# A sliding-window attention block: the row maxima's two bf16 halves written by ScalarE and GpSimd instead of VectorE

## The chip, the cores and the metric

The kernel runs on one core of a Trainium2 chip. A core has five engines with a queue of instructions each, worked off in order: TensorE (PE, with its weight loads as PEld), VectorE (DVE), ScalarE (ACT), GpSimd (POOL) and SyncE (SP, which here only issues DMA transfers). They meet through semaphores. The metric is the device time of one execution in microseconds, the median of several; lower is better.

## The reference

One transformer block on x of 2048 x 640, in f32: a layer norm, then attention and a gated MLP in parallel, and the sum of both with x.

```python
def _A_ref(x, wqkv, wo):                    # H = 32 heads of Dh = 20, window W = 256
    qkv = (x @ wqkv).reshape(B, S, 3, H, Dh).transpose(2, 0, 3, 1, 4)
    q, k, v = qkv[0], qkv[1], qkv[2]
    scores = einsum("bhqd,bhkd->bhqk", q, k) * (Dh ** -0.5)
    scores = where(mask, scores, -1e9)      # 0 <= query - key < 256
    p = softmax(scores, axis=-1)
    o = einsum("bhqk,bhkd->bhqd", p, v)
    return o.transpose(0, 2, 1, 3).reshape(B, S, D) @ wo

def _B_ref(x, w_gate, w_up, w_down):
    return (gelu(x @ w_gate) * (x @ w_up)) @ w_down

xn = _layernorm(x)
return x + _A_ref(xn, wqkv, wo) + _B_ref(xn, w_gate, w_up, w_down)
```

The softmax subtracts each row's maximum before the exponential. That maximum is what the change is about.

## The kernel before, in words

The work comes in three stages. Up to about 60 us: the layer norm, its turn by TensorE and the first projections. From 60 to about 560 us: the attention, with the rest of the projections and part of the MLP as filler. After that: the rest of the MLP and the output products.

The attention goes over 32 units, eight groups of four heads times four chunks of 512 queries. `qs` and `ks` are the stacks of a unit's q and k in SBUF: bf16 parts of q and k in 60 rows each way (q and k are split into upper and lower bf16 parts so that the product is nearly exact), and four rows more (rows 60 to 63). In those four rows the q stack holds the row maximum as two bf16 numbers, an upper part and the rest (rows 60 and 61) and zeros; the k stack holds constants (`ones`, rows 60 and 61) and zeros. A product over all 124 rows then gives score minus maximum at no further cost.

The maxima are taken a unit or more ahead. `max_pair` (line 509) multiplies 32 queries at a time with their 288 keys into PSUM (`ps_m`, line 529), and VectorE adds the mask and takes the maximum of each row (line 533; two rows of the profile each, the reduction into `junk` and the reading of its accumulator into `mx`). Eight pairs make a unit's 16 columns of `mx`. Behind the eighth, the function `negate` writes the two bf16 halves with their sign into `nm` (lines 542 and 543), and line 544 turns `nm` in blocks of 32 x 32 into `mr`, so that queries lie along a row. `max_end` (line 548) copies `mr` into the q stack by four DMA transfers on SP's queue (line 552).

`exp_piece` (line 573) multiplies the stacks (`ps_e`, line 587) and ScalarE takes the exponential into `P` (line 589); `clear` masks the edges on GpSimd (lines 600 and 603); `av_unit` multiplies `P` with v (`ps_o`, line 627), ScalarE copies the two halves out (lines 631 and 632) and GpSimd adds them (line 633). Filler: `save_qk` splits a projection (`pt` and `r`: line 285 on ScalarE, 281 on VectorE, 266 on ScalarE, 267 on GpSimd), `gate_up_fill` computes the MLP's gate (674, 675, 684 on ScalarE; 680, 688, 695 on VectorE), `split_later` splits weights (656, 661), and `x_sums` forms sums on GpSimd (758).

All queues are in the order in which the code is written. `attention` (line 823) counts slots, 14 to a unit (`NS`): in slots 0, 4 and 8 it takes pairs of maxima (four pairs in slot 0, two before and two behind `av_unit`), in slots 2, 4, 6, 8 and 10 score pieces (three, two, two, two, three), loads the k stack three units ahead in slot 9 and the q stack in slot 12, and puts some 2.4 steps of filler behind each slot. `defer(n, fn)` runs fn at the start of the slot n later, `late(fn)` behind the slot's score pieces. The eighth pair of a unit falls into slot 0 of the unit before it, behind `av_unit`; `negate` runs there. `max_end` comes six slots later. PSUM for `ps_m`, `ps_e` and `ps_o` is a ring of six banks: a piece writes the bank that was used six banks before, once its reader has finished.

Of the kernel before, what the change touches and what calls it, by code (L numbers as in the profile page):

```python
# [13 lines left out]
AF = mybir.ActivationFunctionType  # L14
OP = mybir.AluOpType
# [56 lines left out]
def block_kernel(ctx, tc, x, wqk, wv, wgu, wdo, wdl, out):  # L72
    nc = tc.nc
# [64 lines left out]
    def ln_load(t, lp):  # L138
        xi = lp.tile([128, D], F32, name="xi", tag="xi", bufs=8)
        nc.sync.dma_start(xi, x[t * 128:(t + 1) * 128, :])  # L140
        return xi
# [53 lines left out]
    now = [None]  # L195

    def at(slot, fn, *a):
        acts.setdefault(slot, []).append((fn, a))
# [17 lines left out]
    def late(fn, *a):  # L216
        if now[0] is None or now[0] < NS:
            fn(*a)
        else:
            lates.append((fn, a))  # L220
# [9 lines left out]
    def defer(n, fn, *a):  # L230
        if now[0] is None:
            fn(*a)
        else:
            at(now[0] + n, fn, *a)
# [8 lines left out]
    def load_qk(t):  # L243
        raw = wrp.tile([128, KT, 128], F32, name="wr", tag="wr")
        nc.sync.dma_start(raw, wqk[t])
        return raw
# [43 lines left out]
    def load_v(h, res, rpool=None):  # L290
        wh = wvp.tile([128, KT, 320], F32R, name="wvh", tag="wvh")
        wl = wvp.tile([128, KT, 320], F32R, name="wvl", tag="wvl")

        if rpool is not None:
            rall = rpool.tile([128, KT, 320], F32, name="wvall")
            nc.sync.dma_start(rall, wv[h])

        def get(k):
            if rpool is not None:
                return rall[:, k, :]  # L300
            raw = wvp.tile([128, 320], F32, name="wvr", tag="wvr", bufs=2)
            nc.sync.dma_start(raw, wv[h, :, k, :])
            return raw
        raws = [get(0), get(1)]
        yield
        for k in range(KT):
            if rpool is None and 0 < k < KT - 1:
                raws.append(get(k + 1))
            nc.scalar.activation(wh[:, k, :], raws[k], AF.Copy)
            nc.gpsimd.tensor_tensor(out=wl[:, k, :], in0=raws[k], in1=wh[:, k, :].bitcast(F32), op=OP.subtract)  # L310
            if rpool is not None and k + 2 < KT:
                raws.append(get(k + 2))
            yield
        res.append((wh, wl, v_tiles()))
# [26 lines left out]
    def run(*gens):  # L341
        for gen in gens:
            for _ in gen:
                pass
# [84 lines left out]
    with tc.tile_pool(name="lp", bufs=1, side="right") as lp:  # L429
        xs = [ln_load(t, lp) for t in range(2)]  # L430
        wr0 = load_qk(0)
        xs += [ln_load(t, lp) for t in range(2, 4)]
        warm = lp.tile([128, 256], BF, name="warm")[:, 0:128]
        nc.vector.memset(warm, 0.0)
        ps = psd.tile([128, C], F32, name="ps_u", tag="dn")
        for i in range(WARM):
            nc.tensor.matmul(ps[:, 0:128], warm, warm, start=True, stop=True)
        wr5 = load_qk(5)
        prep = load_v(0, v0, lp)
        next(prep)  # L440
        xs += [ln_load(t, lp) for t in range(4, 8)]
        w0, w5, mv1 = first_chunk(xs, wr0, wr5, lp)
        run(prep)
        v0 = v0[0]
        ones = lp.tile([4, 2 * C], BF, name="ones")
        nc.gpsimd.memset(ones, 0.0)
        nc.gpsimd.memset(ones[0:2], 1.0)
        for i in range(NK):
            for j in (0, 2):
                nc.sync.dma_start(ks[i][SR:64, j:j + 2].rearrange("p j t -> p (j t)"), ones)  # L450
        for c in range(1, NC):
            ln_scale(xs[4 * c:4 * c + 4], lp, mv1 if c == 1 else None)
            vs = [proj_v(v0, 4 * c - 4 + i, None if i % 2 else (psm, "mx")) for i in range(4)]
            if c == 1:
                with tc.manual_schedule(engines={mybir.EngineType.PE}):
                    lead = (cost for gen in vs for cost in gen)
                    for _ in range(VLEAD):
                        next(lead)
                    ln_turn(4 * c, xs[4 * c:4 * c + 4])
                    run(lead)  # L460
            else:
                ln_turn(4 * c, xs[4 * c:4 * c + 4])
            if c + 1 < NC:
                xs += [ln_load(t, lp) for t in range(4 * c + 4, 4 * c + 8)]
            if c == 1:
                for i in range(NQ):
                    for j in (0, 2):
                        nc.sync.dma_start(qs[i][SR + 2:64, j:j + 2].rearrange("p j t -> p (j t)"), ones[2:4])
            if c == 2:
                for z in range(4):  # L470
                    band = mask if z == 0 else lp.tile([128, D], F32, name="xi", tag="xi", bufs=8)[:, 0:288]
                    nc.gpsimd.memset(band, 0.0)
                    nc.gpsimd.affine_select(out=band, in_=band, pattern=[[1, 288]], compare_op=OP.is_ge,
                                            fill=NEG, base=32 * z - 1, channel_multiplier=-1)
                    nc.gpsimd.affine_select(out=band, in_=band, pattern=[[-1, 288]], compare_op=OP.is_ge,
                                            fill=NEG, base=256 - 32 * z, channel_multiplier=1)
                    if z:
                        nc.gpsimd.tensor_copy(mask[32 * z:32 * z + 32], band[32 * z:32 * z + 32])
                raws1 = [load_qk(1), load_qk(6)]
            if c < NC - 1:  # L480
                run(*vs)
                run(proj_qk(0, w0, c), proj_qk(5, w5, c))
            else:
                run(*[proj_v(v0, 4 * c - 4 + i) for i in range(VEARLY)])
# [19 lines left out]
    def bank(name):  # L504
        return psr.tile([128, C], F32, name=name, tag=f"ring{next(turn_of) % 6}")
# [3 lines left out]
    def max_pair(u, i):  # L509
        g, c = divmod(u, NC)  # L510
        jj, b = divmod(i, 4)
        q, k = qs[u % NQ], ks[u % NK]
        if i == 0:
            maxes[u] = ap.tile([128, 4, 4], F32, name="mx", tag="mx")
        n = 128 * b + 128 if c == 0 and b < 2 else 288
        pss = [bank("ps_m") for _ in range(2)]
        todo = []
        for h in range(4):
            q0 = 128 * b + 32 * h
            k0 = q0 + 32 - n  # L520
            parts = [(max(0, -k0), n, k, max(0, k0), q0 + 32)]
            if k0 < 0:
                parts.append((0, -k0, ks[(u - 1) % NK], C + k0, C) if c else (0, -k0, k, 0, None))
            todo += [(i_, h, q0, *part) for i_, part in enumerate(sorted(parts, key=lambda p: p[1] - p[0]))]
        for _, h, q0, lo, hi, kt, k0, k1 in sorted(todo, key=lambda p: p[:2]):
            for r, ps in enumerate(pss):
                rows, j = slice(64 * r, 64 * r + SR), 2 * r + jj
                keys = kt[rows, j, k0:k1] if k1 else kt[rows, j, 0:1].to_broadcast([SR, hi])
                nc.tensor.matmul(ps[32 * h:32 * h + 32, lo:hi], q[rows, j, q0:q0 + 32], keys,  # L529
                                 start=True, stop=True, tile_position=(64 * r, 32 * h))  # L530
        for r, ps in enumerate(pss):
            junk = ap.tile([128, 288], BF, name="junk", tag="junk", bufs=2)
            nc.vector.tensor_tensor_reduce(out=junk[:, 0:n], in0=ps[:, 0:n], in1=mask[:, 288 - n:288], scale=1.0,  # L533
                                           scalar=NEG, op0=OP.add, op1=OP.max,
                                           accum_out=maxes[u][:, 2 * r + jj, b:b + 1])
        if i == 7:
            mx = maxes.pop(u)
            nm = ap.tile([128, 2, 4, 4], BF, name="nm", tag="nm")
            mr = maxes[u] = ap.tile([128, 32], BF, name="mr", tag="mr")

            def negate():
                nc.vector.tensor_scalar(nm[:, 0], mx, -1.0, None, op0=OP.mult)
                nc.vector.scalar_tensor_tensor(nm[:, 1], mx, -1.0, nm[:, 0], op0=OP.mult, op1=OP.subtract)
                nc.vector.transpose(mr, nm.rearrange("p z j b -> p (z j b)"))

            late(negate)

    def max_end(u):
        mr = maxes.pop(u)
# [980 lines left out]
```

## Time and profile before

| | |
|---|---|
| median of 3 runs | 1032.23 us (1030.94 to 1032.3) |
| the profiled execution | 1038.09 us |
| its span | 1036.3 us |
| PE busy in the span | 1022.0 us, 99% |
| attention stage | about 60 to 560 us |

The page gives the busy time of each engine as a share of the span. A group of instructions has a line, an engine, an operation, what it writes and reads (`out<-in`), a count, its busy time, the mean of one in ns, and the idle time of the engine before it with what ended it. A timeline row has start and length in us and, in brackets, the idle time before it. A row of the waits has a total, a number of times and the longest. The difference of 1.8 us between the profiled execution and its span lies around the instructions.

### The profile page before, as it was taken

Reading aid. Unit: us, or ns where it says so; the run is one execution under the profiler, and the core shown is the slowest. Engines: PE = TensorE matmul, PEld = TensorE weight load, DVE = VectorE, ACT = ScalarE, POOL = GpSimd, SP = SyncE. Lnnn points to the kernel's source line nnn. Section 1 sums busy time; section 2 is a strip of 40 time slices with the busy share of each in tenths; the row PEclk is TensorE's granted clock in tenths of the full one; section 3 lists DMA queues with packets and bytes.
Section 4 is the critical chain, followed back from the end, with each engine's and each line's share of the span. In section 5 each row is a group of like instructions: output and inputs, shape, how many; then the busy total and the mean of one; then the engine's idle time right before and its main releaser. Section 6 shows DMA issues by size and latency. Waiting matters only on the chain.

```text
span 1036.3 us, 28668 instructions
## 1 busy us (share of the span) xinstructions
PE 1022.0 (99%) x10909; PEld 853.1 (82%) x10909; DVE 718.8 (69%) x2039; ACT 522.2 (50%) x1088; POOL 379.6 (37%) x541
## 2 busy tenths in 40 slices
PE   8999999999999999999999999999999999999998
PEld 8987676777788766777777888888888999999998
DVE  8844655666655665776654778777556879888887
ACT  4444766766666666666676432323224644333332
POOL 5222778886765576666664111110110000000000
PEclk9999999999999998999999999999999999999999
DMA  5642465645333254535423567777127864443342
GB/s 202 190 146 77 120 207 161 196 151 181 124 125 103 90 168 132 157 112 161 135 74 130 166 205 247 248 240 244 67 79 258 261 213 147 136 129 124 112 135 89
DMA packets 109744, 161.81 MB, mean 156 GB/s; under 512 B 18556, under 2 KB 63228, under 8 KB 109608
## 3 DMA queue, kind: packets, MB, share of 16 engines
q1 hardware_dynamic: 108312, 154.09, 46.5%
q10 hardware_dynamic: 1296, 5.90, 1.8%
q8 instruction: 86, 1.41, 0.6%
q14 instruction: 50, 0.41, 0.1%
HBM read 101.78 MB, written 57.80 MB: 154 GB/s over the span
## 4 chain that ended last, share of the span: by engine, by line
PE 84%; DVE 6%; DMA 3%; POOL 3%; ACT 2%; issue 1%; SPq 0%; ACTq 0%; DVEq 0%; POOLq 0%
PE ps_g L971 21%; PE ps_d L111 21%; PE ps L1241 16%; PE ps_e L587 8%; PE ps_v L111 7%; PE ps_o L627 6%; PE ps_m L529 4%; PE ps_g L111 1%; DVE ss L1076 1%; DVE at L1076 1%; PE ps_t L182 1%; DMA hr<-hd 1%; DMA stg<-wtd 1%; DMA hr<-od 1%; ACT at L1195 1%
## 5 line engine op out<-in xcount | busy, mean ns | idle before, releaser
L533 DVE CUSTOM_DVE_ANT_0 junk<-ps_m,mask 128x288 bf16<-128x288 f32 (+2 forms) x512 | 197.7, 441 | 122.1 <-PE ps_m L529 121.2
L589 ACT ACTIVATE P<-ps_e 128x512 f32<-128x512 f32 (+2 forms) x384 | 195.9, 576 | 69.6 <-PE ps_e L587 68.8
L1241 PE MATMUL ps<-wb,at 128*128 128x320 f32 x999 | 156.7, 309 | 1.0 <-DVE xr L1267 0.8
L1241 PEld LDWEIGHTS ps<-wb,at 128*128 128x128 f32 x999 | 148.9, 188 | 2.1 <-issue 1.0
L600 POOL TENSOR_SCALAR_AFFINE_SELECT P<-P 128x512 f32<-128x512 f32 x128 | 84.6, 662 | 89.1 <-ACT P L589 88.8
L587 PE MATMUL ps_e<-qs,ks 124*128 124x128 bf16 (+2 forms) x704 | 108.1, 279 | 4.4 <-DVE mx L533 4.4
L111 PE MATMUL ps_d<-xl,wqh 128*128 128x512 f32 x350 | 106.4, 413 | 0.0
L111 PE MATMUL ps_d<-xh,wqh 128*128 128x512 f32 x350 | 105.9, 412 | 0.0
L111 PE MATMUL ps_d<-xh,wql 128*128 128x512 f32 x350 | 105.4, 411 | 0.0
L587 PEld LDWEIGHTS <-ks 124*128 124x128 bf16 x704 | 50.6, 98 | 51.3 <-issue 33.1
L1241 PE MATMUL ps<-wt,at 128*128 128x320 f32 x552 | 89.3, 309 | 0.4 <-DVE u L1076 0.4
L1241 PEld LDWEIGHTS ps<-wt,at 128*128 128x128 f32 x552 | 82.9, 188 | 0.9 <-DVE u L1076 0.9
L1195 ACT ACTIVATE at<-ss 128x512 fp32r<-128x512 f32 x59 | 37.3, 632 | 91.6 <-DVE ss L1076 91.6
L104 POOL TENSOR_TENSOR wql<-wr,wqh 128x640 fp32r<-128x640 f32 x11 | 17.7, 1610 | 173.4 <-PE ps_g L971 128.0
L603 POOL TENSOR_SCALAR_AFFINE_SELECT P<-P 128x512 f32<-128x512 f32 x112 | 72.1, 654 | 15.6 <-ACT P L589 15.6
L627 PE MATMUL ps_o<-P,v 64*32 64x320 f32 (+5 forms) x2816 | 77.1, 347 | 0.2 <-POOL P L603 0.2
L111 PEld LDWEIGHTS ps_d<-xl,wqh 128*128 128x128 f32 x350 | 64.3, 191 | 12.7 <-issue 2.3
L111 PEld LDWEIGHTS ps_d<-xh,wql 128*128 128x128 f32 x350 | 64.0, 189 | 13.0 <-issue 2.3
L111 PEld LDWEIGHTS ps_d<-xh,wqh 128*128 128x128 f32 x350 | 63.7, 190 | 13.3 <-issue 2.6
L627 PEld LDWEIGHTS ps_o<-P,v 64*32 64x32 f32 x2816 | 67.2, 106 | 4.7 <-POOL P L603 1.4
L267 POOL TENSOR_TENSOR pt<-r,pt 128x512 bf16<-128x512 f32 x40 | 46.9, 1172 | 57.5 <-ACT pt L266 55.4
L529 PE MATMUL ps_m<-ks,qs 60*32 60x96 bf16 (+4 forms) x3008 | 61.3, 244 | 1.3 <-DVE he L680 0.7
(193 smaller groups left out, 1895.9 us busy)
## 6 DMA issues: line engine op xcount, KB each, us to landing
hr<-hd SPq DMA_DIRECT2D x104, 128.0 KB
hd<-he SPq DMA_DIRECT2D x50, 256.0 KB
wr<-wgu SPq DMA_DIRECT2D x27, 320.0 KB
oe<-ob SPq DMA_DIRECT2D x32, 256.0 KB
qs<-qd SPq DMA_DIRECT2D x64, 120.0 KB
ks<-kd SPq DMA_DIRECT2D x64, 120.0 KB
xi<-x SPq DMA_DIRECT2D x16, 320.0 KB
qs<-qd SPq DMA_DIRECT2D x64, 80.0 KB
```

The lines of the kernel that those rows point to most:

```text
L111: nc.tensor.matmul(ps, a(k), b(k), start=n == 0, stop=n == 3 * nk - 1)
L267: nc.gpsimd.tensor_tensor(out=pt[:, l, :], in0=r, in1=pt[:, 1, :], op=OP.subtract)
L529: nc.tensor.matmul(ps[32 * h:32 * h + 32, lo:hi], q[rows, j, q0:q0 + 32], keys, start=True, stop=True, tile_position=(64 * r, 32 * h))
L533: nc.vector.tensor_tensor_reduce(out=junk[:, 0:n], in0=ps[:, 0:n], in1=mask[:, 288 - n:288], scale=1.0, scalar=NEG, op0=OP.add, op1=OP.max ...
L587: nc.tensor.matmul(ps[:, col:col + n], k[0:QROWS, j, kc:kc + 128], q[0:QROWS, j, q0:q0 + n], start=True, stop=True)
L589: nc.scalar.activation(pt[:, j, lo:hi], ps[:, lo:hi], AF.Exp, scale=SCALE)
L600: nc.gpsimd.affine_select(out=a, in_=a, pattern=[[0, 4], [1, 128]], compare_op=OP.is_ge, fill=0.0, base=0, channel_multiplier=-1)
L603: nc.gpsimd.affine_select(out=a, in_=a, pattern=[[0, 4], [-1, 128]], compare_op=OP.is_ge, fill=0.0, base=-1, channel_multiplier=1)
L627: nc.tensor.matmul(halves[h][32 * j:32 * j + 32, q0:q0 + n], v[rows, w0_:w0_ + 32], pts[u, bi][rows, j, col:col + n], start=i == 0, stop=i ...
L971: nc.tensor.matmul(ps, i, j, start=first and n == 0, stop=n == len(work) - 1, skip_group_check=True)
L1195: nc.scalar.activation(hi[:, 3:7], s, AF.Copy)
L1241: nc.tensor.matmul(ps[bank][:, 0:HD], *work[bank][j], start=bank not in begun, stop=final[p, bank] == n and j == len(work[bank]) - 1, skip ...
```

## The change

The function on VectorE goes. The upper half of the maxima is written by ScalarE as a rounding copy (two slots later), the lower by GpSimd as the difference (three slots later), both without a sign, and VectorE keeps the turn (four slots later, behind that slot's score pieces). The sign moves into the k stack: its two rows hold -1 instead of 1, written once.

```diff
         nc.gpsimd.memset(ones, 0.0)
-        nc.gpsimd.memset(ones[0:2], 1.0)
+        nc.gpsimd.memset(ones[0:2], -1.0)
...
             nm = ap.tile([128, 2, 4, 4], BF, name="nm", tag="nm")
             mr = maxes[u] = ap.tile([128, 32], BF, name="mr", tag="mr")
 
-            def negate():
-                nc.vector.tensor_scalar(nm[:, 0], mx, -1.0, None, op0=OP.mult)
-                nc.vector.scalar_tensor_tensor(nm[:, 1], mx, -1.0, nm[:, 0], op0=OP.mult, op1=OP.subtract)
-                nc.vector.transpose(mr, nm.rearrange("p z j b -> p (z j b)"))
-
-            late(negate)
+            d = 1 if now[0] < 0 else 2
+            defer(d, lambda: nc.scalar.activation(nm[:, 0], mx, AF.Copy))
+            defer(d + 1, lambda: nc.gpsimd.tensor_tensor(out=nm[:, 1], in0=mx, in1=nm[:, 0], op=OP.subtract))
+            defer(d + 2, late, lambda: nc.vector.transpose(mr, nm.rearrange("p z j b -> p (z j b)")))
```

Lines 542 to 544 are in the new file the copy, the subtraction and the turn; lines behind stand two lower (587 is 585, 589 is 587, 674 is 672).

ScalarE at the first score pieces, about 92 us of the profile, before: `v` are copies of projections, `ACT_TABLE_LOAD` loads the exponential's table.

```order
L266 ACTIVATE pt<-r 128x512
L285 ACTIVATE pt<-ps_d 128x512
L266 ACTIVATE pt<-r 128x512
L339 ACTIVATE v<-ps_v 128x4x20 x12
L589 ACT_TABLE_LOAD
L589 ACTIVATE P<-ps_e 128x384 x3
```

And now:

```order
L285 ACTIVATE pt<-ps_d 128x512
L266 ACTIVATE pt<-r 128x512
L339 ACTIVATE v<-ps_v 128x4x20 x12
L542 ACTIVATE nm<-mx 128x16
L587 ACT_TABLE_LOAD
L587 ACTIVATE P<-ps_e 128x384 x3
```

The copy of the maxima stands ahead of the table load. ScalarE at about 269 us, in the slots 0 to 4 of a unit of the first chunk, before:

```order
L631 ACTIVATE ob<-ps_o 128x512
L632 ACTIVATE P<-ps_o 128x512
L674 ACTIVATE gs<-ps_d 128x512
L675 ACTIVATE he<-ps_d 128x512
L589 ACTIVATE P<-ps_e 128x384 x4
```

And now:

```order
L629 ACTIVATE ob<-ps_o 128x512
L630 ACTIVATE P<-ps_o 128x512
L542 ACTIVATE nm<-mx 128x16
L672 ACTIVATE gs<-ps_d 128x512
L673 ACTIVATE he<-ps_d 128x512
L587 ACTIVATE P<-ps_e 128x384 x4
```

The copy stands behind the two copies of `ps_o` and ahead of the filler's and the unit's first exponentials. VectorE at the same place, before (an `ISA` row of `junk` is a reduction, one of `mx` its accumulator's):

```order
L533 ISA junk,mx<-ps_m,mask 128x288
L533 ISA mx 128x1
L542 TENSOR_SCALAR nm<-mx 128x16
L543 SCALAR_TENSOR_TENSOR nm<-mx,nm 128x16
L544 STREAM_TRANSPOSE mr<-nm 128x32
L680 SCALAR_TENSOR_TENSOR he<-he,gs 128x512
L533 ISA junk,mx<-ps_m,mask 128x288
L533 ISA mx 128x1
```

And now:

```order
L678 SCALAR_TENSOR_TENSOR he<-he,gs 128x512
L533 ISA junk,mx<-ps_m,mask 128x288
L533 ISA mx 128x1
L533 ISA junk,mx<-ps_m,mask 128x288
L533 ISA mx 128x1
L533 ISA junk,mx<-ps_m,mask 128x288
L533 ISA mx 128x1
L533 ISA junk,mx<-ps_m,mask 128x288
L533 ISA mx 128x1
L544 STREAM_TRANSPOSE mr<-nm 128x32
```

The turn has moved from behind the unit's last reductions to behind the next four. The rows of PE and of SP stand in the same order as before.

## Prediction

> **What bounds the kernel now.** I read the page's first block, then the windows, TensorE's (PE's) waits, the groups that the change touches, and last the timeline at single places. The page's first line says that PE is the bound and that nothing else is near:
>
> ```profile
> PE 1022.0 (99%) x10909; PEld 853.1 (82%) x10909; DVE 718.8 (69%) x2039; ACT 522.2 (50%) x1088; POOL 379.6 (37%) x541
> ```
>
> The change acts in the attention stage alone, 60 to 560 us. Its whole idle time of PE, and the clock around one place (columns: stretch, its length, busy us of PE, PEld, DVE, ACT, POOL, then the granted clock, DMA share, GB/s):
>
> ```profile
> 60.00:560.00 500.00, 494.09 (x7873) 370.60 (x7872) 301.86 (x1203) 317.79 (x685) 329.87 (x477) 0.99 0.45 137
> ...
> 382.00:389.00 7.00, 4.87 (x52) 3.19 (x53) 6.90 (x12) 3.33 (x8) 6.20 (x11) 1.00 0.30 88
> 389.00:396.00 7.00, 6.29 (x34) 3.72 (x34) 4.07 (x18) 3.49 (x7) 1.80 (x2) 0.51 0.39 118
> ```
>
> PE idles 500 - 494.09 = 5.9 us there. Who ended those waits (us, times, longest):
>
> ```profile
> PE ps_e L587 <- DVE mx L533: 4.4, 3, 2.8
> PE ps_m L529 <- DVE he L680: 0.7, 1, 0.7
> PE ps_m L529 <- issue: 0.5, 1, 0.5
> ```
>
> So no change on VectorE (DVE) can win more than 5.9 us of idle time, plus what the clock does afterwards. The three instructions of line 541's function (busy us, mean ns, 32 of each):
>
> ```profile
> L542 DVE TENSOR_SCALAR nm<-mx 128x16 bf16<-128x16 f32 x32 | 25.3, 789 | 1.1
> L543 DVE SCALAR_TENSOR_TENSOR nm<-mx,nm 128x16 bf16<-128x16 f32 x32 | 15.9, 496 | 1.1
> L544 DVE STREAM_TRANSPOSE mr<-nm 128x32 bf16<-128x32 bf16 x32 | 6.8, 212 | 1.1
> ```
>
> Sixteen elements cost more than the turn of 32: the first two stretch. One stretched further than all others:
>
> ```profile
> 383.49 4.74 DVE L542 TENSOR_SCALAR nm<-mx 128x16 bf16<-128x16 f32 x1
> ...
> 383.77 1.31 POOL L633 TENSOR_TENSOR ob<-ob,P 128x512 f32<-128x512 f32 x1
> ...
> 387.56 0.65 POOL L603 TENSOR_SCALAR_AFFINE_SELECT P<-P 128x512 f32<-128x512 f32 x1
> ...
> 389.70 0.75 PE L587 MATMUL ps_e<-qs,ks 124*128 124x256 bf16 x2 [2.83 <-DVE mx L533]
> ```
>
> It ends when GpSimd (POOL) pauses, at 388.21. PE then has waited 2.83 us, and the 7 us behind run at 0.51 of the clock, which loses 7 x 0.49 = 3.4 us. **The event costs 6.2 us.** The profiled execution took 1038.09 us, the median of the runs is 1032.23: 5.9 us apart. I read this as: the timed runs do not have the event. 1038.09 - 6.2 = 1031.9 is then the base.
>
> The Trainium skill ("SBUF — State Buffer", section "Who interferes with whom") says that VectorE and GpSimd share one port pair, which whoever starts first holds for its instruction while the other waits until it ends. The 4.74 us lie over several GpSimd instructions, so the trace goes beyond that rule here; by the rule alone L542 would be at most one GpSimd instruction late, the event would not exist, and the sum would start from 1031.9 as mine does. The skill's "TensorE: Matmul & The Clock Gate" (section "What's actually happening") puts the fall to half rate behind an idle window of about 3.4 us; here 2.83 us were enough. By the page's window the event would be worth 2.8 us only, the base 1035.3 and the sum 1039.4; I go by the clock row.
>
> **Part 1: the two VectorE instructions go.** 25.3 + 15.9 us over 32 units, 1.29 us a unit, leave VectorE. It waits for PE most of the time, so this is worth only what PE waited for VectorE outside the event: 4.4 - 2.8 + 0.7 = 2.3 us, of which the largest piece hangs on GpSimd (part 4) and stays. I take -0.4, between 0 and -1.0.
>
> **Part 2: the copy on ScalarE (ACT).** Its price is in no row. The nearest are a copy of 80 elements and a Sqrt of 4:
>
> ```profile
> L339 ACT ACTIVATE v<-ps_v 128x80 f32<-128x80 f32 x128 | 20.1, 246 | 17.5 <-PE ps_v L111 17.4
> L153 ACT ACTIVATE sq<-mv,one 128x4 f32<-128x4 f32 x3 | 0.9, 298 | 4.8 <-DVE mv L147 4.8
> 299.15 0.65 ACT L339 ACTIVATE v<-ps_v 128x80 f32<-128x80 f32 x4
> ```
>
> Four in 0.65 us: (0.65 - 0.246) / 3 = 0.135 us each when they overlap, which I take; 0 and 0.30 are the ends. ScalarE has the room. The cost is the wait: the copy stands ahead of the unit's first exponentials and cannot start before the sixteenth maximum, and ScalarE works in order. Where the maxima come late, everything behind the copy is late. Unit 13:
>
> ```profile
> 269.64 0.08 DVE L533 DVE_READ_ACCUMULATOR2_ANT mx<- 128x1 f32 x1
> ...
> 268.97 0.60 ACT L674 ACTIVATE gs<-ps_d 128x512 f32<-128x512 f32 x1
> ...
> 269.92 1.29 ACT L589 ACTIVATE P<-ps_e 128x384 f32<-128x384 f32 x3
> ...
> 271.32 0.45 PE L587 MATMUL ps_e<-qs,ks 124*128 124x384 bf16 x2
> 271.52 0.48 PE L111 MATMUL ps_d<-xh,wql 128*128 128x512 f32 x1
> ```
>
> The maxima stand at 269.72; L674 began at 268.97. Behind the copy it begins at about 269.9, 0.95 late, and the two L67x and three exponentials follow without a pause. The third exponential ended at 271.21. Its PSUM bank is taken, six banks on, by the second piece of the row at 271.32, which began at about 271.5. Of the 0.95 us some 0.2 are slack, **0.7 us stop PE**. I did the same for the 31 units (delay of the third exponential, less the slack of the fifth piece). In 22 the slack covers it. In nine it does not: 0.65, 0.81, 0.56, 0.07, 0.74, 0.26, 0.25, 0.14 and 0.52 us, **4.0 us**; 2.9 if the copy took no time and only waited, 5.6 at 0.30 us. The first and the last of the nine:
>
> ```profile
> 93.62 0.08 DVE L533 DVE_READ_ACCUMULATOR2_ANT mx<- 128x1 f32 x1
> ...
> 91.74 1.28 ACT L589 ACT_TABLE_LOAD   x1
> 93.74 1.25 ACT L589 ACTIVATE P<-ps_e 128x384 f32<-128x384 f32 x3 [0.72 <-PE ps_e L587]
> ...
> 95.57 0.45 PE L587 MATMUL ps_e<-qs,ks 124*128 124x384 bf16 x2
> ...
> 504.51 0.08 DVE L533 DVE_READ_ACCUMULATOR2_ANT mx<- 128x1 f32 x1
> ...
> 504.24 0.60 ACT L674 ACTIVATE gs<-ps_d 128x512 f32<-128x512 f32 x1 [0.28 <-PE ps_d L111]
> 505.21 1.26 ACT L589 ACTIVATE P<-ps_e 128x384 f32<-128x384 f32 x3
> ...
> 506.39 0.45 PE L587 MATMUL ps_e<-qs,ks 124*128 124x384 bf16 x2
> ```
>
> In the first the table load of 1.28 us, done by 93.02 and hidden, moves behind the copy: the exponentials start near 95.1 instead of 93.74.
>
> **Part 3: the turn moves.** It stands behind the next four reductions on VectorE and waits for GpSimd. SyncE (SP) issues its rows in order and already waits for the turn; the loads of the next k and q stacks stand behind:
>
> ```profile
> SPq L552 <- DVE mr L544: 37.2, 10, 6.3
> 243.47 0.08 DVE L533 DVE_READ_ACCUMULATOR2_ANT mx<- 128x1 f32 x1
> 242.12 2.59 SPq L552 DMA_DIRECT2D qs<-mr  x4
> 248.47 2.47 SPq L500 DMA_DIRECT2D qs<-qd  x6
> 256.44 0.45 PE L529 MATMUL ps_m<-ks,qs 60*32 60x32 bf16 x32
> PEld L529 <- DMA qs<-qd: 1.4, 2, 0.8
> ```
>
> In that unit the issue moves from 242.1 to about 243.8 (reductions end at 243.55, then 0.21 for the turn), 1.7 us later, and the q loads end their issue at about 252.6 instead of 250.94, 3.8 us ahead of their use. PE waits for such a load at two places now, 0.8 us at most. I take +0.2, between 0 and +4. The maxima's own rows are wanted ten slots later and have room. No DMA is added; SP's rows keep their order.
>
> **Part 4: the subtraction on GpSimd.** Nearest rows: 482 ns at 128 elements and, on the page, 1172 ns at 512 (L267), 1.8 ns an element, so 482 - 112 x 1.8 = 0.28 us at 16. Ends: 0.1 and 0.48. VectorE's reductions cover it, except where VectorE already waits for GpSimd and PE for VectorE:
>
> ```profile
> L661 POOL TENSOR_TENSOR wql<-wr,wqh 128x128 fp32r<-128x128 f32 x75 | 34.7, 482 | 0.6 <-ACT wqh L656 0.6
> 173.73 0.69 DVE L281 TENSOR_TENSOR r<-ps_d,pt 128x512 f32<-128x512 f32 x1 [4.04 <-POOL pt L267]
> 174.84 1.13 PE L587 MATMUL ps_e<-qs,ks 124*128 124x128 bf16 x6 [1.38 <-DVE mx L533]
> ```
>
> There the wait of 1.38 us grows by the subtraction: +0.3, between 0 and +0.5. The sign costs nothing: the same memset writes -1.
>
> **Sum.** 1038.09 - 6.2 - 0.4 + 4.0 + 0.2 + 0.3 = **1036.0 us**, 0.4% above the median of before. Runs of this kernel cannot tell a change under about 0.2% (2.1 us) from none.
>
> **Rivals.** *The delays are absorbed* (same): the maxima in those nine units come earlier than now, since VectorE has less to do, by the 0.5 to 1.0 us that the copy waits. Against it: the removed work stands behind those maxima, not ahead. 1031.9 + 0.1, about 1032. *The event is in the timed runs too*: it vanishes, 1032.23 - 6.2 + 4.1 = 1030.1, at the edge of faster; the 5.9 us between profile and median speak against it. *VectorE's release does more than I grant* (faster): maxima early enough everywhere that part 2 is nothing, and all PE idle outside the event goes, 5.9 - 2.8 = 3.1: 1029.1; it decides where the copy finds its maxima ready in all nine. *The late loads bind* (slower): were a q load to take over 3.8 us to land, PE would wait in most of the twenty later units, 0.2 us each, 1040.
>
> **Numbers.** The forecast 0.37 (its own range 1034.3 to 1038.5), late loads 0.09, absorbed 0.28, event in the timed runs 0.15 (0.09 of it faster), release 0.11. Faster 0.20, same 0.34, slower 0.46. The range, 1029.5 to 1039.0, leaves out most of the late loads and the tail of the release.
>
> **What would show it.** Right: no VectorE row of nm, the turn at 0.21 us; PE waits of 0.3 to 0.8 us ended by ScalarE at L585's score pieces in about nine units, near 95, 109 and 271 us; the first table load after the first maxima; PE's clock unbroken between 60 and 560. Wrong: PE has no new waits there, or the copies start with maxima long ready. The weakest step is the slack in those nine units, read off one execution.

## The result and the profile after

| | before | after |
|---|---|---|
| median of 6 runs each, side by side | 1032.34 us (1030.94 to 1033.1) | 1037.51 us (1035.7 to 1042.3) |
| the profiled execution | 1038.09 us | 1036.38 us |
| its span | 1036.3 us | 1034.6 us |

The ratio after to before is 1.0058, with a 95% interval of 1.0035 to 1.0081: **slower by 0.6%, some 6 us** (the two medians are 5.2 us apart). The two profiled executions alone say the opposite, 1.7 us faster, because that of before has the event at 383 us, worth about 6 us, and most timed runs do not. In 52 timed runs of before, in two further series (one more, far off at a lower clock, left out), three lay at 1036.3 to 1037.6 us, two of them at a mean clock of 0.996 like the 0.997 of the profiled execution, and all others between 1029.6 and 1033.5.

The page's first line of the changed kernel: VectorE gives up 39 us of 719 (4 of them the stretch of the event), and the program gets no shorter by it.

```profile
PE 1021.4 (99%) x10909; PEld 851.9 (82%) x10909; DVE 679.4 (66%) x1975; ACT 526.0 (51%) x1120; POOL 385.4 (37%) x573
```

The three instructions by groups (columns as before):

```profile
L542 ACT ACTIVATE nm<-mx 128x16 bf16<-128x16 f32 x32 | 6.9, 217 | 23.4 <-DVE mx L533 23.4
L543 POOL TENSOR_TENSOR nm<-mx,nm 128x16 bf16<-128x16 f32 x32 | 7.5, 234 | 10.2 <-ACT nm L542 10.2
L544 DVE STREAM_TRANSPOSE mr<-nm 128x32 bf16<-128x32 bf16 x32 | 6.6, 207 | 2.0 <-POOL nm L543 1.9
```

The copy itself is 6.9 us of ScalarE in all. The 23.4 us behind the second bar are what ScalarE stood still for the maxima ahead of it, in order, with everything else of ScalarE behind. Most of this took the place of other idle time: ScalarE's waits for scores (`P` for `ps_e`, 60 to 560 us) fall from 68.8 to 46.7 us. What it costs is only what it makes PE wait.

The windows, for the attention stage and for the place of the event, which is gone: no idle time there, and the full clock.

```profile
60.00:560.00 500.00, 494.19 (x7869) 369.31 (x7868) 261.36 (x1139) 320.94 (x717) 335.11 (x509) 1.00 0.45 137
382.00:389.00 7.00, 7.00 (x164) 5.51 (x162) 3.89 (x17) 4.23 (x8) 7.00 (x11) 1.00 0.72 214
389.00:396.00 7.00, 7.00 (x83) 4.57 (x81) 3.92 (x19) 5.31 (x14) 6.44 (x11) 1.00 0.22 63
```

PE still idles 5.8 us of the 500, as much as before with its event. Who ended its waits now, from the waits between 60 and 560 us:

```profile
PE ps_m L529 <- DMA qs<-qd: 2.6, 5, 0.7
PE ps_e L585 <- DVE mx L533: 1.2, 2, 1.0
PE ps_e L585 <- ACT P L587: 0.4, 2, 0.2
PE ps_m L529 <- issue: 0.3, 1, 0.3
PE ps_m L529 <- ACT P L587: 0.3, 1, 0.3
```

The first row is the new one: before, a load of the q stack (`qs<-qd`) was not among the waits of PE's matmuls in this stage, and among those of its weight loads with 1.4 us at two places, which are now six:

```profile
PEld L529 <- DMA qs<-qd: 3.7, 6, 1.1
```

The waits for ScalarE look small here because much of such a delay stands as a matmul that the record shows busy and that runs late. PE executes the same 10909 matmuls in the same order in both kernels, so I set them side by side by number: where the start of a matmul falls back against the same one of before, time is lost. By that, up to 380 us (of the trace of before, as all such times here) the changed kernel falls 5.5 us behind; at 383 to 396 it wins back 5.7, the event; by 560 us it stands at +0.7. Of the losses up to 380 us, 3.1 us lie at six rows of score pieces behind the copy, 0.5 at a score piece at 374 us (the section on the turn alone shows what holds it up) and 2.3 at three matmul rows that read a new q stack; 0.4 us are won near 175. Between 800 and 900 us, where nothing was changed, the changed kernel wins 1.9 us more; the other kernels win 0.7 to 1.9 us there too, so this belongs to the one execution of before.

The first place behind ScalarE, from the timeline:

```profile
93.49 0.08 DVE L533 DVE_READ_ACCUMULATOR2_ANT mx<- 128x1 f32 x1
93.61 0.21 ACT L542 ACTIVATE nm<-mx 128x16 bf16<-128x16 f32 x1 [2.02 <-DVE mx L533]
93.84 1.28 ACT L587 ACT_TABLE_LOAD   x1
95.14 1.25 ACT L587 ACTIVATE P<-ps_e 128x384 f32<-128x384 f32 x3
95.68 0.33 PE L529 MATMUL ps_m<-ks,qs 60*32 60x128 bf16 x15 [0.26 <-ACT P L587]
```

ScalarE waits 2.02 us for the last maximum, copies in 0.21, and only then loads the exponential's table; the exponentials start at 95.14 instead of 93.74, and PE stops for one of them. The first place of the other kind, SP's rows and PE's:

```profile
142.37 0.20 DVE L544 STREAM_TRANSPOSE mr<-nm 128x32 bf16<-128x32 bf16 x1
142.60 2.61 SPq L550 DMA_DIRECT2D qs<-mr  x4
150.42 4.22 SPq L500 DMA_DIRECT2D qs<-qd  x6
155.82 0.17 PE L529 MATMUL ps_m<-ks,qs 60*32 60x32 bf16 x1 [0.66 <-DMA qs<-qd]
156.63 0.59 PE L529 MATMUL ps_m<-ks,qs 60*32 60x32 bf16 x31 [0.63 <-DMA qs<-qd]
```

And the same place before:

```profile
138.31 0.21 DVE L544 STREAM_TRANSPOSE mr<-nm 128x32 bf16<-128x32 bf16 x1
140.87 2.62 SPq L552 DMA_DIRECT2D qs<-mr  x4
148.71 2.73 SPq L500 DMA_DIRECT2D qs<-qd  x6
153.62 0.82 PE L529 MATMUL ps_m<-ks,qs 60*32 60x32 bf16 x32
```

The turn ends at 142.57 instead of 138.52. Before, SP came to it 2.3 us later; now SP stands ready and waits for it, and issues at 142.60. The q loads behind it start 1.7 us later and take 4.22 us to issue instead of 2.73, so that the last is issued 3.2 us later than before. PE itself comes to the place 1.5 us later, by what it lost earlier. Before, the last load was issued 2.2 us ahead of its use. Now the row that waits for it starts at 156.63, 2.0 us behind the end of the issue at 154.64; by this estimate a load needs some 2.0 us to arrive, and hardly 0.2 us of the lead of 2.2 were slack. How often SP waits for the turn between 90 and 560 us (us, times, longest), where the kernel before had 37.2, 10 and 6.3:

```profile
SPq L550 <- DVE mr L544: 85.1, 25, 6.4
```

### The profile page after: what moved, and what is told of

The parts are those of the page before. It is cut to its first block, busy times and chain, and to the rows that moved or that the text cites. A ratio compares the mean times of both kernels' runs of the same rounds, so it can differ in the third digit from the quotient of the medians.

```text
span 1034.6 us, 28715 instructions
## 1 busy us (share of the span) xinstructions
PE 1021.4 (99%) x10909; PEld 851.9 (82%) x10909; DVE 679.4 (66%) x1975; ACT 526.0 (51%) x1120; POOL 385.4 (37%) x573
## 4 chain that ended last, share of the span: by engine, by line
PE 87%; DMA 3%; DVE 3%; ACT 3%; POOL 2%; issue 1%; SPq 1%; DVEq 0%; ACTq 0%; POOLq 0%
PE ps_g L969 21%; PE ps L1239 21%; PE ps_d L111 19%; PE ps_e L585 7%; PE ps_v L111 7%; PE ps_o L625 6%; PE ps_m L529 3%; PE ps_g L111 1%; ACT P L587 1%; DMA qs<-qd 1%; DMA qd<-pt 1%; PE ps_t L182 1%; PE ps_d L361 1%; DMA wr<-wqk 1%; DVE ss L1074 0%
## 5 line engine op out<-in xcount | busy, mean ns | idle before, releaser
L587 ACT ACTIVATE P<-ps_e 128x512 f32<-128x512 f32 (+2 forms) x384 | 195.2, 574 | 47.7 <-PE ps_e L585 46.7
L529 PE MATMUL ps_m<-ks,qs 60*32 60x96 bf16 (+6 forms) x3008 | 63.3, 244 | 3.4 <-DMA qs<-qd 2.6
```

Source lines behind the costliest of these rows:

```text
L587: nc.scalar.activation(pt[:, j, lo:hi], ps[:, lo:hi], AF.Exp, scale=SCALE)
```

## The experiments

All are compared with the kernel before, run beside them: its median was 1031.17 us (29 runs) for the first four and 1031.91 us (23 runs) for the others.

### ScalarE's copy alone

The kernel before, with a copy of the maxima by ScalarE into a tile that nothing reads, at the place that the change gives it.

```diff
             late(negate)
+            nx = ap.tile([128, 4, 4], BF, name="nx", tag="nx")
+            defer(1 if now[0] < 0 else 2, lambda: nc.scalar.activation(nx, mx, AF.Copy))
```

> The kernel before with the changed kernel's copy on ScalarE added at its place, into a tile that nobody reads; the maxima still go through VectorE. Two-wait theory: only ScalarE's part, 3 to 3.5 us, about 1035.5 us, with PE held at the score pieces near 95, 110 and 271 us. Rival 'late turn alone': 1032.3. Rival 'ScalarE alone': 1037.5.

Measured: 1035.43 us median (12 runs), ratio 1.0037, interval 1.0018 to 1.0056. So the copy alone costs some 3.8 us (1.9 to 5.8 by the interval), as the theory of the two waits had it. PE stops at the predicted places, the first two:

```profile
95.77 0.33 PE L529 MATMUL ps_m<-ks,qs 60*32 60x128 bf16 x15 [0.26 <-ACT P L591]
111.04 0.87 PE L589 MATMUL ps_e<-qs,ks 124*128 124x128 bf16 x4 [0.16 <-ACT P L591]
```

Matmul by matmul it falls back 0.8 us at 95, 0.8 at 110, 0.5 at 213, 0.6 at 271, 0.2 each at 314 and 342 and 0.4 at 506, together 3.5 us, and 1.0 us more at the q load near 154 and 0.5 at matmuls of the maxima near 477. The place near 154 stands in several of the kernels here, and moves by some half a microsecond either way in others (0.6 us later where only the form of L542 is changed); it reacts to nearly anything.

### GpSimd's subtraction alone

```diff
             late(negate)
+            ny = ap.tile([128, 4, 4], BF, name="ny", tag="ny")
+            defer(2 if now[0] < 0 else 3, lambda: nc.gpsimd.tensor_tensor(out=ny, in0=mx, in1=nm[:, 0], op=OP.subtract))
```

> The kernel before with the changed kernel's subtraction on GpSimd added at its place, into a tile that nobody reads. All theories so far give it little: 0 to 0.5 us, 1032.3 to 1032.8. If GpSimd's queue is part of the loss it shows here, as up to 2 us, with VectorE waiting for L267 longer than before near 174 and 232 us.

Measured: 1030.87 us (12 runs), ratio 0.9988, interval 0.9975 to 1.0002. Its group:

```profile
L548 POOL TENSOR_TENSOR ny<-mx,nm 128x16 bf16<-128x16 f32 x32 | 7.0, 220 | 11.4 <-DVE nm L542 10.1
```

220 ns each, and no loss. The prediction's +0.3 us for it does not exist.

### The copy behind the slot's score pieces

The changed kernel, with ScalarE's copy behind the score pieces of its slot instead of ahead of them.

```diff
-            defer(d, lambda: nc.scalar.activation(nm[:, 0], mx, AF.Copy))
+            defer(d, late, lambda: nc.scalar.activation(nm[:, 0], mx, AF.Copy))
```

> The changed kernel with ScalarE's copy of the maxima behind the slot's three score pieces instead of ahead of them. Two-wait theory (ScalarE waits in order for the maxima and holds up the exponentials, about 3.4 us; the later turn holds up SyncE and with it the q loads, about 2.4 us): the first part goes and the second stays, about 1034.5 us, no PE wait for ScalarE at the score pieces, waits for q loads as in the changed kernel. Rival 'ScalarE alone': back to about 1032.3. Rival 'late turn alone': no gain, about 1037.5 or more.

Measured: 1036.53 us (12 runs), ratio 1.0048, interval 1.0031 to 1.0066. Most of the stops behind ScalarE go, and the time does not come back. What takes their place, in PE's waits between 60 and 560 us, at the worst place, and in the windows around it:

```profile
PE ps_m L529 <- DMA qs<-qd: 5.9, 6, 1.9
...
156.78 0.17 PE L529 MATMUL ps_m<-ks,qs 60*32 60x32 bf16 x1 [1.85 <-DMA qs<-qd]
...
150.00:157.00 7.00, 5.10 (x103) 3.69 (x91) 2.48 (x14) 3.40 (x8) 4.03 (x5) 1.00 0.70 224
157.00:164.00 7.00, 6.42 (x69) 4.30 (x69) 3.79 (x17) 3.01 (x8) 3.56 (x5) 0.76 0.44 129
```

The waits for q loads grow from 2.6 to 5.9 us, and behind the longest the clock falls to 0.76 over 7 us (7 x 0.24 x 2 = 3.4 us at half clock). The copy later makes the subtraction and the turn later, and SP with them (its waits for the turn grow from 85.1 to 92.5 us): one cost was exchanged for the other. No theory gave this time; it suggested that the turn's place was a cost of its own, and far more than the 0.2 us of the prediction.

### All three instructions later

The kernel before, with its whole function four slots later.

```diff
-            late(negate)
+            defer(3 if now[0] < 0 else 4, late, negate)
```

> The kernel before with its three VectorE instructions kept together but four slots later, where the changed kernel has the turn; nothing on ScalarE or GpSimd. Two-wait theory: only the late turn's part, 2 to 2.5 us, about 1034.5 us, with PE waits for q loads near 154, 168 and 227 us and none for ScalarE. Rival 'ScalarE alone': 1032.3. Rival 'late turn alone': 1037.5.

Measured: 1047.89 us (5 runs), ratio 1.0146, interval 1.0124 to 1.0168: slower than any theory said. It is no clean test of the turn. Three instructions moved, so the turn ends later still, and near 173 us L542 is stretched again and makes it later by some 2 us more. PE's waits, the stretched row, the chain behind it, and the windows of two stretches at half clock:

```profile
PE ps_m L529 <- DMA qs<-qd: 8.0, 8, 1.2
PE ps_m L529 <- DVE mx L533: 1.7, 1, 1.7
PE ps_m L529 <- DVE r L281: 1.2, 1, 1.2
...
173.17 2.94 DVE L542 TENSOR_SCALAR nm<-mx 128x16 bf16<-128x16 f32 x1
179.85 1.30 SPq L276 DMA_DIRECT2D qd<-pt  x2
183.40 0.60 ACT L285 ACTIVATE pt<-ps_d 128x512 bf16<-128x512 f32 x1 [3.49 <-DMA qd<-pt]
184.10 0.69 DVE L281 TENSOR_TENSOR r<-ps_d,pt 128x512 f32<-128x512 f32 x1 [5.45 <-ACT pt L285]
...
184.00:191.00 7.00, 5.52 (x32) 3.46 (x31) 3.71 (x17) 2.99 (x6) 4.73 (x7) 0.76 0.66 201
413.00:420.00 7.00, 5.16 (x50) 3.55 (x50) 3.53 (x12) 4.70 (x10) 3.97 (x7) 0.76 0.40 121
```

So q loads are not all that stands behind the turn on SP's queue. The store `qd<-pt`, which gives ScalarE its buffer `pt` back, is issued at 179.85 (in the kernel before at 173.72); ScalarE waits 3.49 us for it, VectorE 5.45 us for ScalarE, and PE 1.72 us for VectorE's maxima, the 1.7 us of the second row.

### The turn alone

The kernel before, with the two instructions on `nm` where they were and only the turn four slots later, as in the change.

```diff
                 nc.vector.scalar_tensor_tensor(nm[:, 1], mx, -1.0, nm[:, 0], op0=OP.mult, op1=OP.subtract)
-                nc.vector.transpose(mr, nm.rearrange("p z j b -> p (z j b)"))
 
             late(negate)
+            defer(3 if now[0] < 0 else 4, late, lambda: nc.vector.transpose(mr, nm.rearrange("p z j b -> p (z j b)")))
```

> The kernel before, with both nm instructions left on VectorE where they were, and the turn alone four slots later. Theory (the turn's new place holds up SP's rows and through them the q loads, worth the 2.4 us found in the changed kernel; ScalarE's copy is worth 3.4 us more): 1033.5 us, +0.2%, between 1032.8 and 1034.5; TensorE waits for q loads in the rows of ps_m near 154, 168, 227 and 404 us, together 2 to 4 us, and no wait for ScalarE behind the score pieces near 95, 110 and 271 us. Rival 1 (ScalarE's copy alone carries the loss, the q loads were late by a chain from ScalarE): 1031.2 us, no new wait for q loads. Rival 2 (the 16 us of the kernel with all three instructions moved came from the turn): over 1040 us.

Measured: 1036.38 us (7 runs), ratio 1.0042, interval 1.0027 to 1.0056. **The turn's place alone costs some 4.3 us** (2.8 to 5.8 by the interval), about as much as ScalarE's copy, above the theory's range, and almost twice what I had read from the changed kernel. Nothing else was moved. PE's waits between 60 and 560 us, SP's between 90 and 560, the place near 154, and the one at 374 (377 to 379 in this trace):

```profile
PE ps_m L529 <- DMA qs<-qd: 3.9, 5, 1.3
...
SPq L552 <- DVE mr L546: 91.1, 25, 6.9
...
155.75 0.45 PE L529 MATMUL ps_m<-ks,qs 60*32 60x32 bf16 x31 [0.95 <-DMA qs<-qd]
377.62 0.60 ACT L285 ACTIVATE pt<-ps_d 128x512 bf16<-128x512 f32 x1 [1.38 <-DMA qd<-pt]
378.75 0.87 PE L587 MATMUL ps_e<-qs,ks 124*128 124x256 bf16 x4 [0.53 <-ACT P L589]
```

SP waits for the turn at 25 places, as in the changed kernel, and matmul by matmul PE falls back 1.0 us at 139, 0.8 at 154, 1.0 at 199, 0.6 at 213 and 0.5 at 227, all at matmuls that read a new q stack, 3.8 us. Behind the place of the event come 1.9 us more at a q load at 404, and 0.9 are won back at 420, where the trace of before waits. Another 0.8 us comes at 374 by the second way: the store `qd<-pt` is late, ScalarE waits 1.38 us for its buffer, and PE for the exponentials behind. The changed kernel has the same stop, 0.5 us with 1.07 us of ScalarE's wait for that store; it stands in the four kernels with the late turn and in no other, so it is the turn's and not the copy's. The stops near 95, 110 and 271 are not there.

### The turn ahead of its slot's reductions

The changed kernel, with the turn at the start of its slot.

```diff
-            defer(d + 2, late, lambda: nc.vector.transpose(mr, nm.rearrange("p z j b -> p (z j b)")))
+            defer(d + 2, lambda: nc.vector.transpose(mr, nm.rearrange("p z j b -> p (z j b)")))
```

> The changed kernel, with the turn at the start of its slot, ahead of that slot's four reductions instead of behind them, some 1.5 us earlier. Theory (two terms, ScalarE's order and late q loads): the q loads' term shrinks from 2.4 to about 0.8 us, ScalarE's 3.4 us stay: 1034.8 us, between 1034.0 and 1035.8; the waits for ScalarE near 95, 110 and 271 us as before. Rival (VectorE then waits for GpSimd's subtraction ahead of four reductions, and TensorE for VectorE): 1037 us or more, with new waits of TensorE ended by mx of L533.

Measured: 1038.44 us (6 runs), ratio 1.0063, interval 1.0051 to 1.0075. The rival was right. VectorE now stands still for GpSimd, and reductions that PE needs stand behind the turn; VectorE's row and PE's rows of the waits between 60 and 560 us, and one place:

```profile
DVE mr L544 <- POOL nm L543: 37.7, 26, 3.8
...
PE ps_e L585 <- DVE mx L533: 2.2, 5, 0.7
PE ps_m L529 <- DMA qs<-qd: 1.9, 4, 0.7
...
173.04 0.21 POOL L543 TENSOR_TENSOR nm<-mx,nm 128x16 bf16<-128x16 f32 x1
173.28 0.21 DVE L544 STREAM_TRANSPOSE mr<-nm 128x32 bf16<-128x32 bf16 x1 [3.18 <-POOL nm L543]
173.92 0.76 PE L585 MATMUL ps_e<-qs,ks 124*128 124x256 bf16 x4 [0.61 <-DVE mx L533]
```

In the changed kernel VectorE waited 1.9 us in all at that row, here 37.7. So the chain of three engines is too long for its place: with the turn early VectorE pays, with the turn late SP does.

### GpSimd's half without ScalarE's

The upper half stays on VectorE in the old place (0 mx + mx, in bf16), the lower goes to GpSimd, the sign to the k stack, and the turn comes two slots after the maxima instead of four.

```diff
-            d = 1 if now[0] < 0 else 2
-            defer(d, lambda: nc.scalar.activation(nm[:, 0], mx, AF.Copy))
+            d = 0 if now[0] < 0 else 1
+            late(lambda: nc.vector.scalar_tensor_tensor(nm[:, 0], mx, 0.0, mx, op0=OP.mult, op1=OP.add))
+            defer(d, lambda: nc.gpsimd.tensor_tensor(out=nm[:, 1], in0=mx, in1=nm[:, 0], op=OP.subtract))
-            defer(d + 1, lambda: nc.gpsimd.tensor_tensor(out=nm[:, 1], in0=mx, in1=nm[:, 0], op=OP.subtract))
-            defer(d + 2, late, lambda: nc.vector.transpose(mr, nm.rearrange("p z j b -> p (z j b)")))
+            defer(d + 1, lambda: nc.vector.transpose(mr, nm.rearrange("p z j b -> p (z j b)")))
```

> Half of the change: the lower half by GpSimd and the sign in the k stack as in the change, but the upper half stays on VectorE where it was (as 0 mx + mx, two inputs), and the turn comes two slots after it, at the slot's start. Nothing is on ScalarE. Theory (the change loses by ScalarE's order and the late q loads; relief of VectorE and GpSimd's part are worth nothing): 1031.2 us, within 0.15%, and no event. Rival (relief of VectorE is worth the 0.4 us and more that its waits show, up to 2.3): 1029 to 1030.5 us. Second rival (VectorE waits for GpSimd at the turn): 1033 us or more, with waits of TensorE ended by mx of L533.

Measured: 1030.99 us (12 runs), ratio 0.9997, interval 0.9987 to 1.0008: the same as before. PE's and VectorE's waits between 60 and 560 us, and SP's between 90 and 560:

```profile
PE ps_e L585 <- DVE mx L533: 1.7, 2, 1.5
PE ps_m L529 <- DMA qs<-qd: 0.7, 1, 0.7
...
DVE mr L544 <- POOL nm L543: 13.5, 27, 1.6
...
SPq L550 <- DVE mr L544: 56.6, 16, 6.3
```

VectorE waits 13.5 us for GpSimd and SP waits at 16 places for the turn, and PE notices next to nothing of either. VectorE lost 20 us of work (698.5 us busy against 718.8, 4 of them the event's) and that, too, changed nothing. Of the parts of the change, this leaves ScalarE's copy and the late turn as what costs.

### L542 with two inputs

The kernel before, with the first instruction in the form of the second, the same number from two inputs.

```diff
-                nc.vector.tensor_scalar(nm[:, 0], mx, -1.0, None, op0=OP.mult)
+                nc.vector.scalar_tensor_tensor(nm[:, 0], mx, -2.0, mx, op0=OP.mult, op1=OP.add)
```

> The kernel before, with line 542 as -2 mx + mx, the same number from an instruction with two inputs in SBUF, as line 543 has. Theory (the single event of 4.74 us belongs to the form with one input, which GpSimd's instructions can hold up one after another; the form of line 543 waits for one of them at most): no L542 over 1.3 us in the profiled execution, no stretch at half clock in the attention stage; the median as before, 1031.2 us, within 0.1%, since the event lies in about one timed run in ten only; no run near 1036 to 1038. Rival 1 (any instruction with operands in SBUF can be held up so): a row of L542 over 2 us in some execution, runs of 1036 to 1038 as before. Rival 2 (the two-input form waits more often): L542's mean over 0.79 us and a median over 1032 us.

Measured: 1032.05 us (11 runs), ratio 1.0009, interval 1.0000 to 1.0018. Its longest run was 1035.65, just below where the theory wanted none. No L542 took over 1.38 us in its profiled execution, there is no stretch at half clock in the windows of the old event, and it still waits for GpSimd most of the time:

```profile
L542 DVE SCALAR_TENSOR_TENSOR nm<-mx 128x16 bf16<-128x16 f32 x32 | 21.1, 659 | 1.1
```

Whether the form is what starves stays open. In the five profiled executions with the old form two of 160 took over 2 us (4.74 and 2.94); with two inputs none of 256 did, L543 counted in. That leans one way and proves nothing. It wins no time in any case.

## Why the prediction was right, and where not

Direction and size came out: 1036.0 us foretold, 1037.51 measured, +0.4% against +0.6% (0.35 to 0.81). Point by point:

- **The base.** Right. Most timed runs are without the event, by some 6 us, so a comparison of the two profiled executions would have given the wrong sign. The event is worth 5.7 us matmul by matmul, 6.2 by the windows. It seems to be in the timed runs now and then (three of 52 lie where it would put them; they have no trace), which the prediction had as all or nothing.
- **Part 1, VectorE's relief, -0.4 us.** Nothing measurable: 0.9997 with one of the two instructions gone. One wait behind VectorE near 175 us did get shorter by 0.4 us in the profiled execution, where part 4 had foretold 0.3 more.
- **Part 2, ScalarE's order, +4.0 us.** Right, by mechanism and size. In the changed kernel seven of the nine places are there, foretold 0.65, 0.81, 0.56, 0.74, 0.26, 0.25 and 0.52 us, found matmul by matmul 0.81, 0.77, 0.54, 0.59, 0.17, 0.19 and 0.44; two small ones (0.07 and 0.14) are not. Together 3.5 us, and 3.5 in the copy's own kernel, of the 4.0. The profile itself names only two of these stops as waits for ScalarE, of 0.2 and 0.3 us, where nine of 0.3 to 0.8 were to show. The size is in part luck: the instruction is 0.217 us where 0.135 was taken, and by the prediction's own ends (4.0 at 0.135, 5.6 at 0.30) it would have foretold some 4.8, an estimate between the two. The 3.8 us of the timed runs hold stops near 154 and 477 us that were not foretold.
- **Part 3, the turn, +0.2 us (0 to +4). This is the term that was mis-sized.** Alone it costs 4.3 us, more than its upper end. In the changed kernel 2.3 us stand at q loads up to 380 us, 0.9 at one at 404 and 0.5 at 374, though the copy alone, too, brings 1.0 of the 1.3 near 154. The failed step is the choice of the example: the unit at 243 to 256 us, where the q loads had 5.5 us of lead before and 3.8 after. At 148.71 to 153.62 us the trace of before has a lead of 2.2 us, of which some 2.0 are the load's own time to arrive, and a delay of SP by 1.7 us uses it up. I had reckoned 31 units one by one for ScalarE and one unit for SP. The second way, by the store that frees `pt`, was not in the sum at all. The row "SPq waits for mr" with its 10 places said that SP already stood at the turn in a third of the units, and so that a later turn would pass through; it gives no price, since the half change stands there at 16 places and loses nothing.
- **Part 4, GpSimd, +0.3 us.** The duration was right, the cost not: 220 to 234 ns each, close to the 0.28 estimated, and no cost.
- **The rivals.** *Absorbed* is refuted by the changed kernel itself, where VectorE has less to do and seven of the nine stops are there all the same (the copy alone leaves VectorE its work and cannot tell). *Release* is refuted by the half change, as far as one of the two instructions goes, and by the changed kernel. *Late loads bind*, at 1040 us and 0.09, was nearer the truth in mechanism than its chance: the loads do bind, in four units (near 154, 168, 227 and 404 us) and not in twenty.

So the sum of 4.1 us came near the 5 to 6 measured with part 2 about right, part 3 too small and parts 1 and 4 nothing or close to it. Whether the two costs add up, the runs do not settle: 3.8 and 4.3 alone make 8.1, together they are 6.0 with an interval of 3.6 to 8.4. The 1.0 us near 154 stands in the copy's kernel and, with 0.8, in the turn's, and can hardly be lost twice; that alone would leave some 7. This was reckoned, not tried.

No version beat the kernel before. The half change equals it; the full change loses in each of the three arrangements that were run (turn late, copy late, turn early).

## What to carry to other kernels

An instruction that is moved to another engine takes its wait with it: price it by what stands behind it in that engine's order and by what that makes the bottleneck wait, here 3.5 us of PE, and neither by its length (7 us of copying) nor by the engine's own standing still (23 us, most of it idle time before as well). When a step is moved to a later place, work out the slack of its consumer for every repetition and take the smallest, following the queue past the step itself to whatever is issued behind: here the loads of other units, and the stores that give a buffer back. And before two profiled executions are subtracted, hold each against its own timed runs.

## What the runs showed of the hardware

- A wait of PE of 1.72 us (all three instructions later) or 1.85 us (the copy behind the score pieces) was enough for a stretch of 3.4 us at half clock behind it, and one of 2.83 us for the 7 us at 0.51 of the kernel before; a wait of 1.5 us in the half change and of 1.3 in the turn's kernel left the clock at 1.00. The Trainium skill ("TensorE: Matmul & The Clock Gate", section "What's actually happening") speaks of an idle window of about 3.4 us that runs on its own count. The lengths of the slow stretches agree with such windows, the waits in front of them were shorter.
- VectorE's 16-element instructions take 0.17 us when GpSimd is idle and 0.71 (L542) or 0.66 (L543) most often beside it, and L542 took 2.94 us again in a second kernel. The Trainium skill ("SBUF — State Buffer", section "Who interferes with whom") has the one wait until the other's instruction ends; the common 0.7 us agrees with that (one GpSimd instruction of 0.65), the 2.94 and 4.74 us do not.
- The same q loads took 2.73 us to issue in the kernel before and 4.22 in the changed one, 1.7 us later. Where the subtraction was added they took 3.19 us and came 0.25 us earlier than before, so a later start alone is not the reason. What is, the runs do not tell.
